# Loading the second matrices of experts 3, 4 and 5 in groups of rows, and moving two later loads in the GpSimd queue

## The chip, the core and the metric

One core of one Trainium2 chip runs one program. The metric is the device time of one execution in microseconds (us); where several executions are given, their median. The profile is of one execution. Its engines are PE (matrix multiply), DVE (vector), ACT (scalar), POOL (GpSimd) and SP (sync). The core has 16 DMA engines, which move all data between HBM (the large memory) and SBUF (the on-chip memory, 128 partitions). POOL issues all loads of this kernel but the first five, because these loads also turn fp32 into fp16 on the way; SP issues those five and all stores.

## What is computed

Sliding-window attention over 8 batches and 8 heads feeds a soft mixture of 8 experts. Cut to what matters here:

```python
scores = where(0 <= i - j < 64, q @ k.T / 8, -1e9)      # seq 576, head size 64
x = (softmax(scores) @ v)  as [4608, 512]
logits = x @ phi                                         # 32 slots, 4 per expert
d = softmax(logits, over the 4608 rows)
slot_input = d.T @ x                                     # [32, 512]
for e in range(8):
    h = relu(slot_input[4e:4e+4] @ w1[e])                # w1[e]: 512 x 1024
    slot_out[4e:4e+4] = h @ w2[e]                        # w2[e]: 1024 x 512
c = softmax(logits, over the 32 slots)
out = c @ slot_out                                       # [4608, 512], fp32
```

Every expert's two matrices, 2 MB each in fp32, are needed whole, and no expert's work can start until the attention of all batches is done, since `d` is normalised over all rows.

## The kernel before

The work is one program written out by hand: every engine's order of instructions is the order of the calls in the source.

**Attention, about 0 to 135 us.** A loop over 32 pairs of heads (`for n in range(-1, NP - 1)`, L596) is software-pipelined: in a turn, one pair's keys are transposed, another's scores are taken, a third's weighted values, and so on. In each turn `loads(n)` (L582) issues loads from POOL: k and q (`load_rows`, L83), v (`load_v`, L180), and, at the turns listed in `WSLOTS` (L573), one whole expert matrix by `load_w(i)` (L136). `load_w(0)` to `load_w(6)` load w1 of experts 0 to 6; `load_w(7)` to `load_w(12)` load w2 of experts 0 to 5. Each is one DMA of 128 rows: one row per partition, which for a w2 is two pieces of 4096 bytes in SBUF (8192 bytes each in HBM).

**After the loop, in source order** (L726 to L735): `load_last1` four times (L148) loads the last expert's w1 in quarters into buffers (`w1h`) of the q loads; `shift_v` and `make_ss4` are copies on POOL that later work needs; then `load_w(12)` and five calls of `load_half` (L154, its DMA is L164). `load_half(0..7)` are the eight quarters of w2 of experts 6 and 7: 0 to 3 hold the first 256 output columns (`d` = 0), 4 to 7 the other 256 (`d` = 1); 2, 3, 6 and 7 are expert 7's and go into buffers (`w2h`) of the k loads. Numbers 5, 6 and 7 are issued later, between three calls of `cb_sub` (L530, its instruction is L532), a POOL subtraction that the combine softmax needs.

**The experts** start with `first(0, 0)` (L903; matmuls at L864). `second_first` (L885) multiplies by w2 of experts 0 to 3, `second(d)` (L891) by those of 4 and 5, `second_last(d)` (L899) by those of 6 and 7, for one half of the columns. When a half is done, ACT copies it (L967, L980), and `give` (L940) forms pieces of the output: matmuls at L950, scaling on ACT (L957) or DVE (L955), and a store from SP (L959). The first six stores hold columns of the first half, the next six columns of the second half, both for the first two of four groups of rows; the last six, of 768 KB each, hold both halves.

**How a POOL load waits.** POOL's DMAs take eight completion semaphores in turn, so the issue of one waits until the DMA eight places before it has landed whole (unless that is known already). An instruction behind a waiting issue on POOL waits too. A landing is reported by 16 increments of the semaphore, and the trace has the time of each.

Of the kernel before, what the change touches and what calls it, by code (L numbers as in the profile page):

```python
# [18 lines left out]
def kernel(  # L19
# [10 lines left out]
    nc = tc.nc  # L30
# [63 lines left out]
    w1_t, w2_t = {}, {}  # L94
    for e in range(NRES):
        w1 = pwt.tile([128, NKK, F], FP16, name=f"w1_{e}")
        w2 = pwt.tile([128, NFC, D], FP16, name=f"w2_{e}")
# [32 lines left out]
    def w1_dram(e):  # L130
        return moe_w1[e].rearrange("(p c) f -> p c f", c=NKK)

    def w2_dram(e):
        return moe_w2[e].rearrange("(h p c) d -> p h c d", h=2, c=NFC // 2)

    def load_w(i):  # L136
        second, e = divmod(i, NRES)
        if second:
            nc.gpsimd.dma_start(out=w2_t[e, 0][:, :, :].rearrange("p (h c) d -> p h c d", h=2), in_=w2_dram(e))
        else:  # L140
            nc.gpsimd.dma_start(out=w1_t[e, 0], in_=w1_dram(e))
# [12 lines left out]
    def load_half(i):  # L154
        d, i = divmod(i, 4)
        e, h = last - 1 + i // 2, i % 2
        if e == last:
            if h == 0:
                w2_t[last].append([])
            c = pin.tile([128, 4, DH], FP16, name="w2h", tag="ks")  # L160
            w2_t[last][d].extend(c[:, j, :] for j in range(4))
        else:
            c = w2_t[e, 0][:, 4 * h:4 * h + 4, DH * d:DH * d + DH]
        nc.gpsimd.dma_start(out=c, in_=w2_dram(e)[:, h, :, DH * d:DH * d + DH])  # L164
# [365 lines left out]
    def cb_sub(b, eng):  # L530
        lgT = lgs[b]
        eng.tensor_tensor(out=lgT[:, :, :], in0=lgT[:, :, :],  # L532
                          in1=cbs[b][:, :].unsqueeze(2).broadcast_to([128, 6, 32]), op=ALU.subtract)
# [7 lines left out]
    def cb_turn(b):  # L541
        nc.vector.transpose(ct_all[:, b, :], cbs.pop(b)[:, :, :].rearrange("p i s -> p (i s)"))
# [39 lines left out]
    def loads(n):  # L582
        if n in WSLOTS:
            load_w(WSLOTS[n])
        i, odd = divmod(n, 2)
        if odd:
            if 0 <= i < NG - 4:
                load_k(i + 4)
        elif i > 0:
            shift_v(i - 1)  # L590
            if i + 1 < NG:
                load_v(i + 1)
            if i + 3 < NG:
                load_q(i + 3)
# [128 lines left out]
    b, p = B - 1, NP - 1  # L723
# [7 lines left out]
    make_ss4()  # L731
    nc.gpsimd.tensor_copy(out=ssf, in_=ss)
    load_w(12)
    for i in range(5):
        load_half(i)  # L735
    st_score8(p - 3)
    st_exp8(p - 3)
# [122 lines left out]
    def first(g, f2):  # L860
        ha, _ = bank("ha")
        for kk in range(NKK):
            for j in range(4):
                nc.tensor.matmul(ha[32 * j:32 * j + 32, :], sit[:, kk, :],  # L864
                                 w1_t[4 * g + j][kk][:, 512 * f2:512 * f2 + 512],
                                 start=(kk == 0), stop=(kk == NKK - 1), skip_group_check=True)

        hv = ha[:, :].rearrange("p (x c) -> p c x", c=4)
        if f2 == 0:
            nc.scalar.activation(hs_[:, g, f2], hv, AF.Relu, scale=emask[:, g:g + 1])  # L870
        else:
            nc.vector.tensor_scalar(out=hs_[:, g, f2], in0=hv, scalar1=emask[:, g:g + 1],
                                    scalar2=0.0, op0=ALU.mult, op1=ALU.max)
# [30 lines left out]
    fr_turn(b)  # L904
    cb_max(b - 2)
    cb_sub(b - 2, nc.gpsimd)
    load_half(5)
    cb_turn(b - 3)
    first(0, 1)
    spread(1, act)  # L910
    cb_max(b - 1)
    cb_sub(b - 1, nc.gpsimd)
    load_half(6)
    first(1, 0)
    turn_hidden(0)
    sums(0)
    cb_exp(b - 2)
    cb_max(b)
    cb_sub(b, nc.gpsimd)
    load_half(7)  # L920
    first(1, 1)
    second_first(range(4))
    turn_hidden(1)
# [102 lines left out]
```

## Time and profile before

| what | value |
|---|---|
| time, median of 3 runs (lowest, highest) | 190.96 us (190.25, 191.86) |
| the profiled execution's own time | 190.96 us |
| its span in the profile | 189.2 us |
| busy share PE, DVE, ACT, POOL | 84%, 76%, 69%, 56% |
| read from HBM, written to HBM | 61.93 MB, 9.44 MB |
| DMA busy share, 40 slices of the span | 9 tenths or more in all but the first and the last |

The span is shorter than the execution by 1.8 us, which lie outside what the profile shows. In rows of a timeline the columns are the start in us from the span's beginning, the duration in us, the engine, the source line, operation and tiles, a count after x, and in brackets the idle time ahead and what ended it. In the chain that ended last the columns are the start, the duration, and what the time went to; "DMA w2h" is time from a load's issue to its landing.

### The profile page before, as it was taken

What the parts mean: (1) busy time and instruction counts of PE and PEld (TensorE: products, weight loads), DVE (VectorE), ACT (ScalarE), POOL (GpSimd) and SP (SyncE); (2) the same over time, 40 slices, a digit from 0 to 9 for tenths busy, and PEclk for the clock granted to TensorE, in tenths of its full rate; (3) what the DMA queues carried; (4) which work ended last, traced back from release to release, by engine and by line L of the source; (5) the groups of instructions that cost most, each with busy time, mean ns of one, the idle gap of its engine ahead of it and who ended that gap; (6) DMA issues with size and microseconds to landing.
All of it is one profiled execution on the core that took longest, in us unless ns stands there. A gap on an engine that the chain in (4) does not pass through costs nothing.

```text
span 189.2 us, 6815 instructions
## 1 busy us (share of the span) xinstructions
PE 158.2 (84%) x2890; PEld 114.9 (61%) x2890; DVE 143.8 (76%) x356; ACT 129.6 (69%) x250; POOL 105.9 (56%) x178
## 2 busy tenths in 40 slices
PE   7966989989999998999999999889898975869400
PEld 2555878876876877787677868657653443544000
DVE  5888688888888898899889889988866520989600
ACT  5666787897787788688788778965772532689500
POOL 7945976976869494798849839460764610000000
PEclk9999999999999999999999999999999997899955
DMA  6999999999999999999999999999999999999996
GB/s 165 216 185 184 187 183 225 176 222 181 185 223 181 212 188 185 215 187 210 195 182 212 192 198 199 208 211 192 218 210 211 209 195 180 258 353 344 406 417 265
DMA packets 63614, 41.46 MB, mean 219 GB/s; under 512 B 38880, under 2 KB 59872, under 8 KB 62688
## 3 DMA queue, kind: packets, MB, share of 16 engines
q0 software_dynamic: 56560, 30.35, 116.2%
q1 hardware_dynamic: 7024, 10.68, 16.4%
q8 instruction: 22, 0.36, 0.7%
q14 instruction: 8, 0.07, 0.1%
HBM read 61.93 MB, written 9.44 MB: 377 GB/s over the span
## 4 chain that ended last, share of the span: by engine, by line
PE 35%; DVE 31%; DMA 20%; issue 4%; ACT 3%; POOL 1%; DVEq 0%; SPq 0%; ACTq 0%
DMA w1h<-in_moe_w_dram 10%; DVE m L391 9%; DMA w2h<-in_moe_w_dram 7%; DVE x_b L459 5%; PE a_m L386 5%; DVE rt L405 3%; PE a_q L340 3%; PE a_s L412 3%; PE a_m L382 3%; PE a_s L418 3%; PE a_k L340 3%; PE cp L950 3%; DVE m L401 2%; DMA w<-in_q_dram 2%; PE a_v L397 2%
## 5 line engine op out<-in xcount | busy, mean ns | idle before, releaser
L391 DVE TENSOR_REDUCE m<-a_m 128x8 f16<-128x1024 f32 x32 | 39.0, 1220 | 0.0
L425 ACT ACTIVATE pt<-a_s 128x1024 f16<-128x1024 f32 x32 | 32.8, 1024 | 7.8 <-PE a_s L418 7.6
L359 POOL COPY qb<-qp 64x288 int32<-64x288 int32 x54 | 22.8, 423 | 20.8 <-ACT qp L356 18.1
L477 ACT COPY xt<-a_k 128x576 f16<-128x576 f16 x28 | 17.9, 638 | 12.7 <-PE a_k L473 12.7
L459 DVE TENSOR_TENSOR x_b<-a_v,rc 128x640 f16<-128x640 f32 x31 | 25.6, 824 | 1.1
L351 ACT ACTIVATE kT<-a_k 128x576 f16<-128x576 f16 x31 | 20.3, 655 | 0.6 <-PE a_k L340 0.6
L405 DVE TENSOR_TENSOR rt<-a_v,kind 36x256 f16<-36x256 f32 x30 | 12.8, 428 | 9.7 <-PE a_v L404 9.1
L955 DVE TENSOR_SCALAR w<-cp,rcs 128x256 f32<-128x256 f32 (+1 forms) x27 | 13.8, 567 | 8.2 <-PE cp L950 8.1
L180 POOL DMA_DIRECT2D v<-in_v_dram x16 | 20.0, 1249 | 0.0
L190 POOL COPY v<-v 64x576 int32<-64x576 int32 x16 | 10.6, 662 | 16.7 <-DMA v<-in_v_dram 16.1
L386 PE MATMUL a_m<-kT,qb 128*128 128x128 f16 x256 | 19.8, 220 | 0.0
L412 PEld LDWEIGHTS <-kT 128*128 128x128 f16 x288 | 18.6, 98 | 1.8 <-issue 1.4
L412 PE MATMUL a_s<-qb,kT 128*128 128x128 f16 x256 | 19.6, 219 | 0.0
L418 PE MATMUL a_s<-rt,lh 128*128 128x256 f16 x128 | 19.2, 273 | 0.4 <-DVE rt L405 0.4
L356 ACT ACTIVATE qp<-a_q 128x576 f16<-128x576 f16 x27 | 18.0, 668 | 1.6 <-PE a_q L340 1.5
L386 PEld LDWEIGHTS <-qb 128*128 128x128 f16 x256 | 14.6, 98 | 7.3 <-issue 5.2
L340 PE MATMUL a_q<-ident_h,qs 96*64 96x96 f16 x384 | 15.1, 207 | 2.7 <-DVE a_q L237 1.4
L449 PE MATMUL a_v<-v,pt 128*64 128x65 f16 x558 | 15.1, 195 | 0.6 <-DVE rt L405 0.4
L957 ACT ACTIVATE w<-cp,rcs 128x256 f32<-128x256 f32 (+1 forms) x27 | 12.8, 544 | 3.6 <-PE cp L950 3.1
L340 PEld LDWEIGHTS <-qs 96*64 96x64 f16 x384 | 12.4, 109 | 4.4 <-issue 3.8
L340 PE MATMUL a_k<-ident_h,ks 96*64 96x96 f16 x384 | 14.2, 210 | 0.1
L449 PEld LDWEIGHTS <-pt 128*64 128x64 f16 x576 | 13.2, 111 | 1.1 <-issue 0.4
(194 smaller groups left out, 346.0 us busy)
## 6 DMA issues: line engine op xcount, KB each, us to landing
w<-in_moe_w_dram POOLq DMA_DIRECT2D x13, 1024.0 KB, 16.0
v<-in_v_dram POOLq DMA_DIRECT2D x16, 288.0 KB, 12.9
out_dram<-w SPq DMA_DIRECT2D x6, 768.0 KB, 7.1
ks<-in_k_dram POOLq DMA_DIRECT2D x15, 288.0 KB, 13.2
qs<-in_q_dram POOLq DMA_DIRECT2D x15, 288.0 KB, 12.7
out_dram<-w SPq DMA_DIRECT2D x7, 384.0 KB, 4.8
w1h<-in_moe_w_dram POOLq DMA_DIRECT2D x4, 256.0 KB, 16.2
w<-in_moe_w_dram POOLq DMA_DIRECT2D x4, 256.0 KB, 14.8
```

Source lines behind the costliest of these rows:

```text
L180: nc.gpsimd.dma_start(out=v1s[b % 2][:, c, 0:Dh], in_=v[b].rearrange("h s d -> (h s) d").rearrange("(c p) d -> p c d", p=128)[:, c, :])
L340: nc.tensor.transpose(tq[64 * hf:64 * hf + 64, RP * r:RP * r + RP], src[0:RP, h + hf, Dh * r:Dh * r + Dh], ident_h[0:RP, 0:RP])
L351: nc.scalar.activation(kTs[p % NK][:, 64:64 + S], turned(a_kh), AF.Copy, scale=QKS)
L359: nc.gpsimd.tensor_copy(out=qbs[p % NQ][:, :, :, :].rearrange("p i l x -> p (i l x)").bitcast(mybir.dt.int32) .rearrange("p (i l x) -> p i ...
L386: nc.tensor.matmul(a_m[:, i // 4, 128 * (i % 4):128 * (i % 4) + 128], qblock(p, i), kwindow(p, i), start=False, stop=True, skip_group_chec ...
L391: nc.vector.reduce_max(m.rearrange("p e j -> p j e"), a_m[:, :, :].rearrange("p l (j e x) -> p (l j) e x", e=2, x=128), axis=AXX)
L405: nc.vector.tensor_tensor(out=rts[p % NR][64:100, :].rearrange("p (e x) -> p e x", e=2), in0=t_[64:100, :].unsqueeze(1).broadcast_to([36, ...
L412: nc.tensor.matmul(at(i), kwindow(p, i), qblock(p, i), start=(i % 4 == 0), stop=False, skip_group_check=True)
L418: nc.tensor.matmul(a_s[:, i // 4, 128 * (i % 4):128 * (i % 4) + 256], lh[:, i // 2, :], rt[:, :], start=False, stop=True, skip_group_check ...
L425: nc.scalar.activation(st_pt(p)[:, 0:8, :].rearrange("p i x -> p (i x)"), a_s[:, :, :], AF.Exp, scale=XS)
L449: nc.tensor.matmul(a_v[r0:r0 + 64, hf, 65 * (i // 2):65 * (i // 2) + 65], pt[:, i, 64 * hf:64 * hf + 64], rhs, start=True, stop=True, skip ...
L459: nc.vector.tensor_tensor(out=xbs[b][:, :, 128 * hp:128 * hp + 128].rearrange("p c (l d) -> p l c d", l=2), in0=avv[:, :, :, 0:64], in1=rc ...
```

## The change

`load_w(10)`, `load_w(11)` and `load_w(12)`, the w2 of experts 3, 4 and 5, become two, three and three DMAs, each of some rows. For expert 4 the last eight rows are taken in two steps, first a quarter of each piece (`c` 0) and then the other three quarters. Nothing that is computed changes. Beside that, `load_half(3)` and `load_half(4)` move from before the tail of the attention into the places where 5 and 6 were, behind the first and the second of the three `cb_sub`, and 5, 6 and 7 all follow the third.

```diff
+    def rows(a, b, c0=0, c1=4):
+        return slice(a, b), slice(c0, c1)
+
+    PARTS = {10: [rows(0, 116), rows(116, 128)],
+             11: [rows(0, 120), rows(120, 128, 0, 1), rows(120, 128, 1, 4)],
+             12: [rows(0, 116), rows(116, 120), rows(120, 128)]}
+
     def load_w(i):
         second, e = divmod(i, NRES)
-        if second:
+        w2 = w2_t[e, 0][:, :, :].rearrange("p (h c) d -> p h c d", h=2)
+        if i in PARTS:
+            for r, cc in PARTS[i]:
+                nc.gpsimd.dma_start(out=w2[r, :, cc], in_=w2_dram(e)[r, :, cc])
+        elif second:
             nc.gpsimd.dma_start(out=w2_t[e, 0][:, :, :].rearrange("p (h c) d -> p h c d", h=2), in_=w2_dram(e))
         else:
             nc.gpsimd.dma_start(out=w1_t[e, 0], in_=w1_dram(e))
...
     load_w(12)
-    for i in range(5):
+    for i in range(3):
         load_half(i)
...
     cb_sub(b - 2, nc.gpsimd)
-    load_half(5)
+    load_half(3)
...
     cb_sub(b - 1, nc.gpsimd)
-    load_half(6)
+    load_half(4)
...
     cb_sub(b, nc.gpsimd)
-    load_half(7)
+    for i in range(5, 8):
+        load_half(i)
```

On POOL the program has five DMAs more than before; on the other engines it has the same instructions in the same order.

## The prediction

> **What bounds the kernel now.** I read the page's slices first (is the DMA system ever idle?), then the chain that ended last in order of time, then POOL's and PE's timelines around it, and last the increments that report each landing.
>
> ```profile
> DMA  6999999999999999999999999999999999999996
> GB/s 165 216 185 184 187 183 225 176 222 181 185 223 181 212 188 185 215 187 210 195 182 212 192 198 199 208 211 192 218 210 211 209 195 180 258 353 344 406 417 265
> ```
>
> The DMA engines are busy in every slice. Each byte that a load writes is two read, so 200 GB/s is 400 read: the stores at the end, at 406 and 417, run at the same pace. The kernel is a queue of transfers from start to end.
>
> ```profile
> 124.44 0.66 POOL w L139
> 125.11 19.44 DMA w1h<-in_moe_w_dram
> ...
> 144.82 13.73 DMA w2h<-in_moe_w_dram
> ...
> 158.60 0.40 PE op L899 x4
> 159.00 0.59 PE rp L705 x5
> 159.59 1.95 PE cp L950 x9
> 161.55 1.21 PE op L891 x8
> ```
>
> From 125 to 158.6 us the end hangs on loads that stand in that queue for 13 to 20 us. At 158.6 the last load of the first half of the columns lands; only then can output be formed.
>
> ```profile
> 157.25 0.29 PE L899 MATMUL op<-w2h,hT 128*32 128x256 f16 x4 [1.04 <-DMA w2h<-in_moe_w_dram]
> 158.60 0.40 PE L899 MATMUL op<-w2h,hT 128*32 128x256 f16 x4 [1.05 <-DMA w2h<-in_moe_w_dram]
> ```
>
> PE is through with the rest by 154.6 and waits for each quarter in turn, so compute has cover here.
>
> ```profile
> 133.55 0.66 POOL L190 COPY v<-v 64x576 int32<-64x576 int32 x1 [7.33 <-DMA v<-in_v_dram]
> ...
> 134.88 1.06 POOL L148 DMA_DIRECT2D w1h<-in_moe_w_dram  x2
> 135.92 0.55 POOL L695 MEMSET v<- 128x512 f16 x1
> ...
> 143.59 0.74 POOL L164 DMA_DIRECT2D w2h<-in_moe_w_dram  x1 [3.22 <-DMA w<-in_moe_w_dram]
> ...
> 146.86 0.52 POOL L532 TENSOR_TENSOR lgT<-lgT,nm 128x192 f32<-128x192 f32 x1
> ...
> 153.50 0.78 POOL L164 DMA_DIRECT2D w2h<-in_moe_w_dram  x1 [2.65 <-DMA w<-in_moe_w_dram]
> ```
>
> POOL is blocked by landings (the eight semaphores): the last quarter is issued at 153.50, when w2 of expert 5 has landed.
>
> Now the increments of one landing, which show what the rows above hide. The last load's sixteen come at 159.7, 159.8, 159.9, 160.2, 160.2, 160.7, 161.0, 161.9, 162.1, 162.4, 162.6, 163.2, 163.3, 163.4, 163.6 and 163.9 us (mean 161.75). The engines are 4.2 us apart, as they were when the w2 of expert 4 landed (139.1 to 143.3), so here the queue is 4.2 us deeper on one engine than on another. The last store's sixteen come at 187.8 to 188.2 (mean 187.94). The latest engine therefore works 188.2 - 163.9 = 24.3 us on stores without a break; the earliest has 187.8 - 159.7 = 28.1 us for the same bytes and idles 3.8 of them; on the mean an engine idles 187.94 - 161.75 - 24.3 = 1.9 us, waiting for output that PE may only form when the latest engine has delivered.
>
> **The change, part by part.** The profiled execution took 190.96 us (span 189.2 and 1.8 around it), which is the median, so sums against it hold for the median.
>
> 1. *Price of a row.* Last increments of the w2 of experts 3 and 4 are at 138.4 and 143.3: 4.9 us for eight rows on each engine, 0.61 us a row.
>
> 2. *Rows moved.* No load of before has a row count that sixteen does not divide, so the trace does not show how 116, 120, 12, 8 or 4 rows are dealt out. I take it that an engine still gets eight in order: 116 fill fourteen engines and half of the fifteenth, 120 fill fifteen, and the remainders go one row to an engine. Then 12 + 8 + 12 = 32 rows (19.5 us of one engine's time) leave one or two engines and are spread over four to twelve others, one to four rows each (0.6 to 2.4 us). The bytes are the same; only where they queue differs.
>
> 3. *What that is worth.* The end is the latest engine's last load plus 24.3 us. Levelled perfectly, all end at 161.75 and the end comes at 186.05 instead of 188.2: -2.15. If the two latest engines are relieved and nothing else, the third latest (163.4) decides: -0.5. The spare rows fit between: four rows on the earliest engine give 159.7 + 2.4 = 162.1. Nothing in the trace names the engines, so neither end is nearer; I take the middle, -1.3. From below: if late engines get the spare rows, up to +2.4 (a rival).
>
> 4. *Are stores early enough?* The first store is issued at 161.0, 2.4 us after the fourth quarter lands (158.6). That quarter's increments run from 154.4 to 158.6, so it gains the same as the last. With the stores of the first half (18 pieces of 128 KB, 2.3 MB, some 6 us at 400 GB/s) in the queue, the engines stay busy while the other quarters finish.
>
> 5. *Five more DMAs in the queue.* A w1h quarter (32 KB an engine to read) takes 1.23 us on the earliest engine (140.4, 141.6, 142.9, 144.1); four are 4.93, a w2 of the same bytes 4.9. A DMA more costs under 0.02 us, five 0.1: +0.1.
>
> 6. *Five more issues on POOL.* 0.53 to 0.78 us each by L148 and L164, 2.7 to 3.9 in all. After 117.2 POOL has 1.14 us idle ahead of its next copies, after 124.4 the 7.33 us above: hidden. Without that cover the copies for the next q block, and PE behind them, would be later by 0.6.
>
> 7. *The semaphores move on by five.* Expert 7's first w1 quarter waits for the w2 of expert 1 (landed 126.7), the second for expert 2's (131.6); the shift of v behind them waits until 133.5 anyway: nothing. The fourth quarter waits for expert 3's (at most 138.4; issued at 135.4 before), so the memset and the copies behind it, which PE's L705 at 140.08 reads, end at 139.4 to 140.9 instead of 137.85: 0 to 0.8 us on PE. PE then reaches L899 at 154.6 to 155.4 and still waits there. Expert 5's parts are issued from about 140.9 to 144 instead of 138.16, behind more than 5 us of queued w1: nothing on the path.
>
> 8. *The moved quarters.* Numbers 3 and 4 now stand behind the first and second `cb_sub`, 5 to 7 behind the third. Their waits (first w1 quarters 145.8 to 148.3, then expert 5's parts) put the subtractions at about 146.8, 148.4 and 150.3, as before (146.86, 148.78, 150.34); in the old order the first would stand behind an issue waiting until 147.1. Quarters 5 to 7 are issued at about 153.2 to 154.8. The earliest engine then has work until 155.7 plus its spare rows. Price 0 if that covers the start of a transfer, at most 1 us if not; I take 0, as it is the engines with spare time that would run dry.
>
> Sum: -1.3 + 0.1 = -1.2, so 189.8 us.
>
> The Trainium skill speaks against small transfers ("DMA: Bandwidth & Descriptors", in "Anatomy of one DMA" and "Rules for kernel authors"): a DMA from POOL has a fixed part of about 2 us, and under 64 KB one pays mostly overhead. If that part were paid one after another, five would make +10 us, an estimate from that page; the quarters of step 5, queued one behind another, paid 0.02, so the trace does not agree for queued loads.
>
> **Rivals.**
>
> *The rows are dealt out by divisors.* If an engine count must divide the row count, 116 = 4 x 29 goes to four engines: 29 rows are 17.7 us instead of 4.9, +12.8 on these, and twice that for an engine that gets both 116s. Time 203.8 to 216.5. For it: every load of before has a count that sixteen divides. Against: nothing in the trace. The skill states this rule ("DMA: Bandwidth & Descriptors", "Why a DMA increments its semaphore by 16 and not by 1"), and beside it an exception measured on trn2 by which some POOL copies keep sixteen shares with the last engines short, which is what step 2 takes; no run here shows either.
>
> *Spare rows on late engines* (the other side). The eight latest engines lie within 2 us, and an engine that is last and gets one row from each remainder ends 4 x 0.61 = 2.4 us later: 193.4. From the first net row on the last engine it is slower; at three rows it is over 1%.
>
> *Nothing moves.* A third late engine keeps the 163.4 to 163.9: 190.5 to 191.0.
>
> **How the numbers follow.** Levelling in part or whole 0.50 (189.8, its own range 188.8 to 190.5); nothing 0.18; spare rows on late engines, or a wait of steps 7 and 8 that shows, 0.19 (191.6 to 193.4); divisors 0.13 (203.8 up). The range of 8 in 10 leaves out the divisors and the edges: 188.7 to 193.5. 1% is 1.9 us, about what a measurement of this kernel can tell from no change. Faster by more needs nearly the whole 2.15: 0.22, under half of the first case. Slower by more: the divisors, and about 0.15 of the third: 0.28. Within 1%: 0.50.
>
> **What would show it.** Right: the last quarter's increments end at 162 to 163 instead of 163.9 and lie closer together; the first store is issued 0.5 to 2 us earlier than 161.0; L899's waits stay. An expert matrix in 116 rows landing 13 us later than its neighbours would show the divisors; a last landing after 163.9, the spare rows misplaced; `cb_sub` rows after 151, or gaps in the DMA share at 153 to 158, steps 7 and 8 wrong.

## The result, and the profile after

| kernel | median, us | ratio to before, 95% interval |
|---|---|---|
| before (6 runs) | 190.82 | |
| the change (6 runs) | 214.29 | 1.121 (1.117 to 1.125) |
| the change again, on another occasion | 214.19 | 1.122 (1.119 to 1.126) |

The change makes the kernel 12% slower, outside the range given. The execution of it that was profiled first ran at a granted PE clock of 0.56 instead of 0.90 and took 247.48 us, so the ratio leaves it out and all rows below are from the second occasion, an execution of 213.89 us, span 212.1 (in the numbering of the changed kernel, 13 or 14 lines on: L150 and L152 are `load_w`, L161 `load_last1`, L177 `load_half`, L545 `cb_sub`, L912 `second_last`).

The slices of its page, 5.3 us each:

```profile
DMA  6999999999999999999999999983479528999997
GB/s 177 203 184 194 183 214 184 217 182 192 214 183 220 177 203 193 206 193 184 216 185 206 202 213 180 182 160 62 89 116 167 92 53 106 147 312 343 375 417 294
```

In slices 28 and 29 and again in 32 and 33 the DMA engines are busy for 2 to 5 tenths and move 53 to 92 GB/s, half or less of the 180 GB/s and more of the slices before. The queue that was never idle in the kernel before now is, twice. The stores at the end look as before. The chain that ended last, in order of time:

```profile
123.65 0.68 ACT qp L369
...
125.22 28.84 DMA w<-in_moe_w_dram
...
154.34 1.13 POOL w L150 x2
155.47 1.54 POOL w L177 x2
...
157.59 0.74 POOL w2h L177
158.35 0.46 POOL lgT L545
158.81 22.51 DMA w2h<-in_moe_w_dram
181.37 0.41 PE op L912 x3
```

The quarter that opens the output (number 3, issued at 158.81) lands at 181.3 instead of 158.6: 22.7 us, and the whole span is 22.9 longer. So next to nothing is lost after it. POOL's timeline shows where it was:

```profile
131.83 0.56 POOL L161 DMA_DIRECT2D w1h<-in_moe_w_dram  x1 [4.09 <-DMA w<-in_moe_w_dram]
...
149.68 0.53 POOL L161 DMA_DIRECT2D w1h<-in_moe_w_dram  x1 [12.38 <-DMA w<-in_moe_w_dram]
150.20 0.54 POOL L708 MEMSET v<- 128x512 f16 x1
150.80 1.33 POOL L711 COPY v<-ss 32x128 f16<-32x128 f16 x4
...
152.44 1.30 POOL L150 DMA_DIRECT2D w<-in_moe_w_dram  x1
...
176.21 0.78 POOL L177 DMA_DIRECT2D w<-in_moe_w_dram  x1 [11.12 <-DMA w<-in_moe_w_dram]
```

POOL stands 12.4 us behind the landing of expert 3's 116 rows and 11.1 us behind that of expert 5's, and PE behind POOL:

```profile
151.14 1.39 PE L718 MATMUL a_v<-ct_all,v 128*128 128x128 f16 x5 [10.04 <-POOL v L711]
...
176.41 1.86 PE L904 MATMUL op<-w,hT 128*32 128x256 f16 x15 [9.10 <-DMA w<-in_moe_w_dram]
...
180.00 0.40 PE L912 MATMUL op<-w2h,hT 128*32 128x256 f16 x4 [0.60 <-DMA w2h<-in_moe_w_dram]
181.37 0.41 PE L912 MATMUL op<-w2h,hT 128*32 128x256 f16 x4 [0.96 <-DMA w2h<-in_moe_w_dram]
```

In the kernel before, PE waited about 1 us for each quarter and at most 0.5 us at a time elsewhere between 139 and 160 us; now it first waits 10.0 and 9.1 us, for a copy that stands behind a POOL issue and for expert 5's matrix itself.

Why these landings are late, the sixteen increments of each tell (us, from the trace; the change):

```
v, issued 115.95             129.2 129.3 129.8 129.9 130.0 130.1 130.2 130.4 132.5 132.6 132.7 133.0 133.7 134.2 134.5 135.4
expert 3, 116 rows (118.08)  129.5 129.7 130.2 130.5 132.9 132.9 133.0 133.5 133.9 134.5 134.8 135.7 147.5 147.7 148.1 149.1
expert 4, 120 rows (125.22)  131.4 135.2 135.4 136.4 137.7 138.0 138.1 138.6 139.5 139.9 140.7 141.0 152.4 152.6 153.0 154.1
expert 5, 116 rows (152.44)  155.3 155.3 155.3 155.3 155.3 155.4 155.4 155.4 155.4 155.4 155.4 160.0 174.3 175.3 175.5 175.9
```

Twelve engines are through with the 116 rows almost as soon as they reach them. The other four need 17.5 to 18.7 us, counted from 130.0 to 130.4: these are the four increments of the v load that no early increment of the 116 rows follows. That fits all the 116 rows on four engines: 29 rows each, 29 x 0.61 = 17.7. Of the 120 rows one engine has none (131.4). Expert 5's 116 rows are issued late, and the late engines still have the first 116 and what queued behind them to finish (their last w1 quarter ends at 157.7 to 159.3): 174.3 to 175.9.

### The profile page after: what moved, and what is told of

Its sections match the earlier page's. It is cut to its first block, busy times and chain, and to the rows that moved or that the text cites. A ratio compares the mean times of both kernels' runs of the same rounds, so it can differ in the third digit from the quotient of the medians.

```text
span 245.7 us, 6822 instructions
## 1 busy us (share of the span) xinstructions
PE 225.4 (92%) x2890; PEld 160.3 (65%) x2890; DVE 149.0 (61%) x356; ACT 132.6 (54%) x250; POOL 110.1 (45%) x183
## 4 chain that ended last, share of the span: by engine, by line
PE 79%; DMA 9%; DVE 5%; ACT 2%; issue 1%; POOL 0%; DVEq 0%; ACTq 0%
PE a_m L399 10%; PE a_s L425 10%; PE a_s L431 9%; DMA w2h<-in_moe_w_dram 9%; PE a_k L353 6%; PE a_q L353 6%; PE a_m L395 6%; PE a_v L462 5%; PE a_k L486 5%; PE cp L964 5%; PE a_m L210 2%; PE a_q L500 2%; PE a_k L425 1%; PE a_v L411 1%; PE a_q L572 1%
## 5 line engine op out<-in xcount | busy, mean ns | idle before, releaser
L372 POOL COPY qb<-qp 64x288 int32<-64x288 int32 x54 | 22.9, 425 | 66.5 <-ACT qp L369 65.1
L438 ACT ACTIVATE pt<-a_s 128x1024 f16<-128x1024 f32 x32 | 32.8, 1024 | 28.4 <-PE a_s L431 25.7
L425 PEld LDWEIGHTS <-kT 128*128 128x128 f16 x288 | 29.2, 132 | 3.4 <-issue 1.6
L431 PE MATMUL a_s<-rt,lh 128*128 128x256 f16 x128 | 30.9, 404 | 0.0
L425 PE MATMUL a_s<-qb,kT 128*128 128x128 f16 x256 | 30.6, 292 | 0.0
L399 PE MATMUL a_m<-kT,qb 128*128 128x128 f16 x256 | 28.3, 275 | 0.0
L418 DVE TENSOR_TENSOR rt<-a_v,kind 36x256 f16<-36x256 f32 x30 | 12.8, 428 | 25.1 <-PE a_v L417 25.0
L399 PEld LDWEIGHTS <-qb 128*128 128x128 f16 x256 | 20.0, 118 | 10.9 <-issue 9.8
L462 PE MATMUL a_v<-v,pt 128*64 128x65 f16 x558 | 21.4, 228 | 0.3 <-DVE rt L418 0.3
L353 PE MATMUL a_q<-ident_h,qs 96*64 96x96 f16 x384 | 21.1, 254 | 0.3 <-DVE a_q L250 0.3
L462 PEld LDWEIGHTS <-pt 128*64 128x64 f16 x576 | 19.3, 135 | 1.2 <-issue 0.9
L431 PEld LDWEIGHTS <-lh 128*128 128x128 f16 x128 | 16.7, 137 | 3.4
L486 PE MATMUL a_k<-ident_h,x_b 128*128 128x128 f16 x140 | 18.1, 285 | 0.0
```

The costliest lines, as they stand in the source:

```text
L353: nc.tensor.transpose(tq[64 * hf:64 * hf + 64, RP * r:RP * r + RP], src[0:RP, h + hf, Dh * r:Dh * r + Dh], ident_h[0:RP, 0:RP])
L372: nc.gpsimd.tensor_copy(out=qbs[p % NQ][:, :, :, :].rearrange("p i l x -> p (i l x)").bitcast(mybir.dt.int32) .rearrange("p (i l x) -> p i ...
L399: nc.tensor.matmul(a_m[:, i // 4, 128 * (i % 4):128 * (i % 4) + 128], qblock(p, i), kwindow(p, i), start=False, stop=True, skip_group_chec ...
L425: nc.tensor.matmul(at(i), kwindow(p, i), qblock(p, i), start=(i % 4 == 0), stop=False, skip_group_check=True)
L431: nc.tensor.matmul(a_s[:, i // 4, 128 * (i % 4):128 * (i % 4) + 256], lh[:, i // 2, :], rt[:, :], start=False, stop=True, skip_group_check ...
L438: nc.scalar.activation(st_pt(p)[:, 0:8, :].rearrange("p i x -> p (i x)"), a_s[:, :, :], AF.Exp, scale=XS)
```

## Experiments

The theory, "divisors" below, is the rival of the prediction that came true: a load goes to as many engines as the largest number up to 16 that divides its row count, and where that is less than 16, to the engines that follow on from where the last such load stopped ("round-robin" below). Its rival, "waits", is that the five more DMAs, through the eight semaphores, and the moved quarters starve the queue.

**The same DMAs with even groups; the order alone.** `again` is the change itself. `even_groups` keeps the number of the DMAs and their places and changes only how many rows each has:

```diff
-    PARTS = {10: [rows(0, 116), rows(116, 128)],
-             11: [rows(0, 120), rows(120, 128, 0, 1), rows(120, 128, 1, 4)],
-             12: [rows(0, 116), rows(116, 120), rows(120, 128)]}
+    PARTS = {10: [rows(0, 112), rows(112, 128)],
+             11: [rows(0, 112), rows(112, 128, 0, 1), rows(112, 128, 1, 4)],
+             12: [rows(0, 96), rows(96, 112), rows(112, 128)]}
```

`order_only` has `PARTS = {}` with the quarters where the change has them.

> The changed kernel once more, for a profile at a full clock. Divisors (a load goes to as many engines as the largest number up to 16 that divides its row count, so 116 rows go to four engines with 29 rows each): each of the two 116-row loads has twelve increments close together and four about 18 us later (29 rows at 0.61 us), and the second starts on engines that the first has made late. Waits (five more DMAs and the moved quarters starve the queue through the eight semaphores): the sixteen increments of a 116-row load lie within some 5 us, and the gaps are in POOL's issues. Time 213 to 215 us by both.

> As many DMAs in the same places and the quarters moved as in the change, but every group has a row count that 16 divides: 112 and 16; 112, a quarter of 16 and the rest of these; 96, 16 and 16. Divisors: sixteen engines share every load, so the time falls back to 189.5 to 192 us. Waits, or a fixed price for small transfers: still 205 to 214 us, since the number of DMAs, their sizes and their places in POOL's queue are about those of the change.

> The row groups taken out, only the moved quarters 3 to 7 left. Divisors: within 1% of before, 189.5 to 192.5 us. Waits: a part of the loss stays, 195 us or more.

Measured: 1.122 (1.119 to 1.126), 1.0016 (0.9993 to 1.0038) and 1.0005 (0.9973 to 1.0036). These are the ratios of `again`, `even_groups` and `order_only`. With row counts that 16 divides, the whole loss is gone, with the same number of DMAs, the same semaphores and the same order. POOL in `even_groups`:

```profile
131.48 0.55 POOL L161 DMA_DIRECT2D w1h<-in_moe_w_dram  x1 [4.44 <-DMA w<-in_moe_w_dram]
...
138.21 0.53 POOL L161 DMA_DIRECT2D w1h<-in_moe_w_dram  x1 [3.28 <-PE a_k L486]
...
146.84 0.52 POOL L545 TENSOR_TENSOR lgT<-lgT,nm 128x192 f32<-128x192 f32 x1
...
152.26 0.77 POOL L177 DMA_DIRECT2D w<-in_moe_w_dram  x1 [0.81 <-DMA w<-in_moe_w_dram]
153.03 0.75 POOL L177 DMA_DIRECT2D w2h<-in_moe_w_dram  x1
154.76 0.74 POOL L177 DMA_DIRECT2D w2h<-in_moe_w_dram  x1 [0.98 <-DMA w<-in_moe_w_dram]
```

POOL's waits are there, and PE has no wait for POOL behind them; it waits 1.25 us at most, for landings. (The second row names PE, but it fits the landing of expert 3's 112 rows at 137.7: the same issue went out at 135.4 in the kernel before.) The theory "waits" falls as a cause of its own.

**One uneven load at a time.** Expert 3's alone in 116 and 12 rows; then expert 4's alone in 120 and 8, 119 and 9, 100 and 28; the quarters in the order of before.

```diff
+    PARTS = {10: [rows(0, 116), rows(116, 128)]}     # one_116
+    PARTS = {11: [rows(0, 120), rows(120, 128)]}     # one_120
+    PARTS = {11: [rows(0, 119), rows(119, 128)]}     # one_119
+    PARTS = {11: [rows(0, 100), rows(100, 128)]}     # split_100
```

> Only expert 3's second matrix in groups (116 and 12 rows), the quarters in the old order. Divisors: four engines get 29 rows instead of 8, 21 x 0.61 = 12.8 us later, less one row's 0.6 that the others gain and what the late engines can make up in the stores: 200 to 204 us, and four increments of the 116-row load 13 us or more behind the others. Waits: one more DMA moves the semaphores by one, 190 to 192 us.

> Before, with only expert 4's load in 120 and 8 rows. Divisors: 120 goes to fifteen engines with eight rows each, as all have before; one engine gets none and shows its increment some 5 us ahead; 8 rows add one row (0.6 us) on eight engines. The end moves by 0 to +0.6 us: 190.6 to 191.7. Eight rows in order on the first engines, as the prediction had it, gives the same.

> One row less: 119 and 9 rows. Divisors: 119 = 7 x 17 goes to seven engines with 17 rows each, so seven increments come 9 x 0.61 = 5.5 us later than with eight rows and nine come early. The end follows the latest of the seven: 194 to 196.5 us. Eight rows in order: 119 fill fourteen engines and seven rows of a fifteenth, 190.5 to 191.7.

> Only expert 4's load in 100 and 28 rows. Divisors: 100 goes to ten engines with ten rows each and 28 to fourteen with two, so six increments of the 100 rows come 5 us or more ahead of the ten; engines in both get twelve rows, +2.4 us: 191 to 193.3 us. Sixteen shares with the last engines short (the exception that the Trainium skill has): seven rows to fourteen engines and two to a fifteenth, so only one or two increments come early, and 190.5 to 191.6 us.

| run | ratio, 95% interval | increments of the first group |
|---|---|---|
| one_116 | 1.058 (1.0546 to 1.0615) | twelve at 129.4 to 135.2, four at 147.0 to 149.2 |
| one_120 | 1.0023 (0.9998 to 1.0047) | one at 134.9, fifteen at 139.6 to 143.1 |
| one_119 | 1.0333 (1.0299 to 1.0368) | nine at 134.7 to 139.4, seven at 146.5 to 149.1 |
| split_100 | 1.0136 (1.0091 to 1.0181) | six at 135.8 to 138.7, ten at 141.4 to 145.0 |

116, 119, 120 and 100 rows go to 4, 7, 15 and 10 engines: the largest divisors up to 16. One row fewer than 120 costs 3.1% where 120 costs nothing measurable. `one_119` came out at 197.3 us, 0.8 above the expected range, and `split_100` at 193.4, 0.1 above. The Trainium skill states this rule and, beside it, an exception for some POOL copies in which 100 partitions fill engines 0 to 14 ("DMA: Bandwidth & Descriptors", "Why a DMA increments its semaphore by 16 and not by 1"); these loads, with two pieces a row, follow the rule: ten engines, not fifteen. A load of one piece a row, in `four_more` below, does not.

The count of packets says the same a second way. These are lines of the DMA view of before, `one_116`, `one_119`, `one_120` and `split_100`:

```profile
DMA packets 63614, 41.46 MB, mean 219 GB/s; under 512 B 38880, under 2 KB 59872, under 8 KB 62688
```

```profile
DMA packets 64334, 41.46 MB, mean 207 GB/s; under 512 B 39600, under 2 KB 60592, under 8 KB 63408
```

```profile
DMA packets 63950, 41.46 MB, mean 213 GB/s; under 512 B 39216, under 2 KB 60208, under 8 KB 63024
```

```profile
DMA packets 63662, 41.46 MB, mean 219 GB/s; under 512 B 38928, under 2 KB 59920, under 8 KB 62736
```

```profile
DMA packets 63758, 41.46 MB, mean 217 GB/s; under 512 B 39024, under 2 KB 60016, under 8 KB 62832
```

The bytes are equal, the packets are 720, 336, 48 and 144 more, all of 4 bytes. 16 of each are the increments of the one more DMA. The rest is what comes out if every engine left out runs through as many 4-byte packets as a working engine has pieces (two a row): 12 x 58 + 4 x 2 = 704, 9 x 34 + 7 x 2 = 320, 1 x 16 + 8 x 2 = 32, 6 x 20 + 2 x 4 = 128. The fit is exact in all four. In the change 1568 more packets have 4 bytes, and the same sum gives 1568 (1488, and 16 for each of the five more DMAs).

**Which engines: the second 116.** Experts 3 and 5 in uneven groups, expert 4 whole, the quarters as in the change; only the last twelve rows of expert 3 differ, in two DMAs either way:

```diff
-    PARTS = {10: [rows(0, 116), rows(116, 120), rows(120, 128)],             # together
+    PARTS = {10: [rows(0, 116), rows(116, 128, 0, 2), rows(116, 128, 2, 4)], # apart
              12: [rows(0, 116), rows(116, 128)]}
```

> Experts 3 and 5 each with a 116-row load, expert 4 whole, quarters moved as in the change. Expert 3's other rows go as 4 and 8: with round-robin (a load that does not fill sixteen engines takes engines following on from where the last such load stopped) 4 + 4 + 8 come back to the start, so the second 116 goes to the same four engines as the first. Round-robin and divisors: about the change's own time, 211 to 215 us, the four late increments of the second 116 about 25 us behind where they would be. With engines chosen afresh each time: the same.

> As the run before, also three DMAs for expert 3, but its other twelve rows go in two halves of twelve rows each. Round-robin: 4 + 12 + 12 stop twelve engines on, so the second 116 starts on four engines that the first has left alone and is not queued behind it: 4 to 8 us faster than the run before, 205 to 209 us. Engines chosen afresh each time (always the same four): the same time as the run before within 1%.

Measured 214.78 and 209.72 us: 1.1257 (1.1218 to 1.1296) and 1.0984 (1.0947 to 1.1021), 5.1 us apart, as round-robin has it; `apart` is 0.7 us above its expected range. The Trainium skill describes such a round-robin ("DMA: Bandwidth & Descriptors", "Why a DMA increments its semaphore by 16 and not by 1"); the 5.1 us agree. POOL in `together` and in `apart`:

```profile
149.81 1.87 POOL L149 DMA_DIRECT2D w<-in_moe_w_dram  x2 [9.64 <-DMA w<-in_moe_w_dram]
...
177.67 1.48 POOL L176 DMA_DIRECT2D w2h<-in_moe_w_dram  x2 [14.42 <-DMA w<-in_moe_w_dram]
```

```profile
149.51 1.88 POOL L149 DMA_DIRECT2D w<-in_moe_w_dram  x2 [10.38 <-DMA w<-in_moe_w_dram]
...
172.31 1.48 POOL L176 DMA_DIRECT2D w2h<-in_moe_w_dram  x2 [8.85 <-DMA w<-in_moe_w_dram]
```

Both issue the second 116 at 149.8 or 149.5, go on with what stands behind it, and wait from about 163 until it has landed; with four other engines that is 5.4 us sooner (172.0 instead of 177.4). It is still late, since POOL had waited 10 us for the first 116 before it issued the second. The eight semaphores put the two delays one behind the other here; that they would otherwise have run side by side is not shown.

**Can the rule be used to level the engines?** `level` takes a quarter of the width of expert 4's load as 119 and 9 rows, `mislevel` as 9 and 119, `four_more` an eighth as 116 and 12, each with the rest whole.

```diff
+    PARTS = {11: [rows(0, 119, 0, 1), rows(119, 128, 0, 1), rows(0, 128, 1, 4)]}  # level
+    PARTS = {11: [rows(0, 9, 0, 1), rows(9, 128, 0, 1), rows(0, 128, 1, 4)]}      # mislevel
+    PARTS = {11: [rows(0, 116, 0, 1, 0, 1), rows(116, 128, 0, 1, 0, 1),           # four_more: the last
+                  rows(0, 128, 1, 4, 0, 1), rows(0, 128, 0, 4, 1, 2)]}            # two numbers cut h
```

> Before, with only expert 4's load changed: a quarter of it as 119 rows (7 engines with 17 rows each) and 9 rows (9 engines with one), the other three quarters whole. In rows of the whole width, seven engines then have 10.25 (1.4 us more work) and nine have 6.25 (1.1 us less), and the round-robin comes back to its start. If the seven are the seven that are early in the profile of before: the last load's last increment comes about 1.1 us earlier and the end with it, 189.0 to 190.3 us. If they are late ones: up to 1.4 us later, 191.5 to 192.5. If the end does not follow the latest engine: 190.8.

> The run before the other way round: the 9 rows first, then the 119, so the nine engines come first and the seven after them. It should be slower by as much as that run is faster: 191.5 to 192.5 us if that one is 189.0 to 190.3. If both are at 190.8 within 0.3%, the end does not follow the latest engine.

> An attempt at a faster kernel. The four engines that take the first 116 rows were early ones in every trace so far. Here only one eighth of the width of expert 4's second matrix goes as 116 and 12 rows, the rest whole: four engines get 2.6 rows more (1.6 us), twelve get 0.9 rows less (0.5 us). If the latest engine is among the twelve, the last increment comes 0.5 us earlier and the time is 190.2 to 190.6 us; if an early engine with 1.6 us more becomes the latest, 191 us or more.

Measured 1.0017 (0.9989 to 1.0046), 1.0085 (1.0055 to 1.0114) and 1.0002 (0.9985 to 1.0020), medians of 191.21, 192.68 and 190.86 us. None is faster, and `mislevel` is slower, 0.2 us more than expected. In the profiled execution of `level`, at 192.21 us one of the slower ones, the last quarter's increments are at 159.4 to 165.4 us: three engines stay early and two are later than any in before, so the seven that got more were not the seven early ones. `mislevel` ends at 165.2. What `level` was meant to show, that levelled engines end sooner, is left open: no run levelled them, as the trace names no engine.

`four_more` shows something else: the rule does not hold there. The sixteen increments of its 116 rows are at 135.0 to 138.6 us and those of the load before at 134.4 to 138.0, all 0.3 to 0.7 later; no four stand out, where 29 rows of an eighth of the width would have put four 2.2 us later. The DMA view agrees:

```profile
DMA packets 63806, 41.46 MB, mean 219 GB/s; under 512 B 38944, under 2 KB 60064, under 8 KB 62880
```

There are 64 more packets of 4 bytes than before, 48 of them the increments of three more DMAs. Four engines with 29 rows would leave 12 x 29 + 4 x 1 = 352 more; eight rows to an engine in order, as step 2 of the prediction had it, leave 16: eight on the engine without a row, four on the one with half its rows, and four beside the 12 rows. It is 16. So these rows were dealt out evenly, and `four_more` tests no levelling. What sets this load apart is that a row is one piece of 1024 bytes; in `level` it is two such pieces, and there the count fits the divisors (352 more, 32 of them increments). No other run has rows of one piece in a number that sixteen does not divide, so this one case is all that tells the condition.

## Why the prediction was wrong

It failed at step 2, *rows moved*: "I take it that an engine still gets eight in order". The runs show 29 rows on four engines instead. Steps 3 and 4 then priced a levelling that did not happen, and the forecast -1.2 became +23.3. The dealing that it assumed does occur, in `four_more`, but for rows of one piece, and the loads of the change have two.

The rival "the rows are dealt out by divisors" named the mechanism and the bounds, 203.8 and 216.5 us, between which the result lies, but had 0.13. The prediction itself said that no run showed either case, and still gave the cases that rest on step 2 together 0.87 and left the divisors out of the range. With no row to decide, the two should have stood about even, and the range should have reached 216.5.

The size of the loss, by the rival's own terms: 21 rows more at 0.61 us are 12.8 us. `one_116` loses 11.1 us (201.93 against 190.86): its four engines were early ones, as far as the increments of the v load before let one tell, and the landing of expert 3's w2 moves from 138.4 to 149.2, 10.8. In the change the second 116 adds the rest: expert 5's landing moves from 153.2 to 175.9, 22.7, and the end by 22.9. The prediction's "twice that for an engine that gets both" is right for three engines: the five uneven loads ahead of it take 4 + 12 + 15 + 8 + 8 = 47 engines in turn and stop one short of the start, so by the round-robin the second set of four overlaps the first by three. The increments fit: one of its four, 174.3, is earlier than the others, and one engine of the first set is done at 160.0.

Step 1 was right: 0.61 us a row gives 17.7 us for 29 rows, against the 17.5 to 18.7 measured.

Step 3's formula held: the end is the latest engine's last load plus 24.3 us. From the last quarter's last increment to the last store's it is 24.4 in the change (186.7 to 211.1), 24.3 in `one_116` (174.7 to 199.0), 24.4 in `one_119` (169.7 to 194.1), 24.5 in `even_groups` (164.5 to 189.0), and 24.1 to 25.0 in the other experiments.

Step 5 was right as far as can be told: `even_groups` has five more DMAs, the smallest of 32 KB, and a ratio of 1.0016 (0.9993 to 1.0038); +0.1 us was forecast and 0.3 measured, not told from none. The "10 us" by a fixed price for each is excluded.

Steps 6 to 8 held where no engine gets too many rows: in `even_groups` the three `cb_sub` start at 146.84, 149.09 and 150.92 (forecast 146.8, 148.4 and 150.3) and the last three quarters are issued at 152.3 to 154.8 (153.2 to 154.8). Step 7's wait, the fourth w1 quarter behind expert 3's landing, was priced at 0 to 0.8 us on PE. With that landing at 149.1 it became 12.4 us on POOL and 10.0 on PE: the wait was found, and its price hung on step 2.

## What to carry to other kernels

The row count of a load can decide how many DMA engines it gets. For the loads of two pieces a row here it is the largest divisor up to 16: 128, 112, 96 and 16 rows run on all sixteen, 119 on seven and 116 on four, at 0.61 us for every row of a w2 that an engine has too many. For rows of one piece the single case seen, 116 rows in `four_more`, was dealt out eight to an engine. Before a load is cut by rows, work out the share of one engine for each piece, and read it back from the increments of its landing: a few of them far behind the rest are engines with too much. Where no row of a profile decides between two ways in which hardware could share out work, a small chance for the dear one is a guess; give the range to both.

## What the runs showed of the hardware that was not expected

Engines that a load leaves out do not seem to be free of it: the counts above come out if each runs through as many 4-byte packets as the others have pieces. In `one_116` twelve engines with none of the 116 rows show their increments 0.5 us later, on the mean, than those of the v load before, so it is cheap.

Whether a row is one piece or two seems to decide how its load is dealt out: 116 rows went to four engines in `one_116` (two pieces of 4096 bytes a row) and, eight to an engine, to fifteen in `four_more` (one piece of 1024), both with the conversion to fp16.

Nine of the sixteen engines are 2.7 us behind the other seven, on the mean, when the last load lands in the kernel before (161.9 to 163.9 against 159.7 to 161.0), though every load there has a row count that 16 divides. Why is not settled by any run here; by the prediction's estimate it costs 1.9 us of idle time.
